# One scaling pass with a running minimum over the scores, and a new order of the work

## The chip, the cores and the metric

One NeuronCore of a Trainium2 chip runs the whole program. The metric is the time of one execution on the device, in microseconds (us); shorter is better. Engines are named as in the profile: PE (TensorE, matrix products; PEld is its weight load), DVE (VectorE), ACT (ScalarE), POOL (GpSimd) and SP (SyncE, which here only issues DMAs).

## The reference

Four batches, eight heads, 576 positions, 64 dimensions per head, all fp32. Queries and keys are rotated by position, then each head is an ordinary softmax attention, and the result goes through a feed-forward network (FFN) with a gate:

```
scores = (1/8) * q_rot @ k_rot^T
scores = scores - max(scores)
attn   = exp(scores) / (sum(exp(scores)) + 1e-9)
x      = attn @ v                                  # heads side by side: 2304 x 512
h      = x @ w_in                                  # 512 -> 2048
out    = (h * clip(h + 3, 0, 6) / 6) @ w_out       # 2048 -> 512
```

## The kernel before

The 2304 rows are cut into 18 tiles of 128 rows; a tile has 8 heads, so there are 144 head-tiles, called heads below. Tile 0 runs in fp32. For the rest every operand is split into a high and a low fp16 part (line 253 or 257 makes the high part, line 265 or 270 the low one), and a product is the sum of three fp16 products: high by high, high by low, low by high.

A head of tiles 1 to 17 (`attention`, line 599) goes through these steps. PE computes the scores S into PSUM, 128 rows by 576 keys (line 570; 573 for the two tiles that lie in two batches). DVE takes the negated maximum of each row (L614). A one-column operation on DVE or POOL turns it into the bias of the exponential, maximum times the row's scale `sig` plus ln 16 (L617). ACT takes the exponential in place, with the sum of the row (L621). ACT or DVE writes its high fp16 part into P16 (L628 or L630), DVE the low part (L632). A DMA issued by SP transposes P16 into PT, and PE multiplies PT by v (L588). S has two buffers in PSUM, P16 four (`NP16`) and PT three (`NPT`). After eight heads `emit_x` divides by the row sums, splits x and transposes it for the FFN.

The FFN works on blocks: tiles 0, 1, 2 and 3 alone, then seven blocks of two tiles. `ffn_h` (L867) computes a slice of h as twelve products in a row, `gate` (L881, L888) applies the gate and splits g (its low part is L898 on POOL), and `ffn_o` (L929) adds six products at a time to the output. The first product of a block of two tiles, the "first wide product" below, has 256 columns where those before have 128; it needs x of tiles 4 and 5. Up to then w_in and w_out are read as 64-bit numbers, decoded on ACT, POOL (L503, L509) and DVE (L517), and split (L265 and others).

All engines run their instructions in the order in which the Python code issues them, and that order is planned. Each step is a generator that yields the engine it wants and an assumed duration; class `Emission` keeps a clock for each engine, lets the waiting step of lowest priority number go first, and chooses for an operation that may run on two engines (`choose`) the one with the smaller sum of queue, duration and a bias from the table `CFG`. `CFG` also holds the priorities and `lead`: a head may be issued only while its number is at most `lead` above the count of FFN units done. So a number in this table, or an assumed duration, changes nothing but the order and the engine.

Of the kernel before, what the change touches and what calls it, by code (L numbers as in the profile page):

```python
# [19 lines left out]
LN_ES = 2.772588722239781  # L20
EPS_ES = 1.6e-8
# [8 lines left out]
NP16 = 4  # L30
NE = 2
# [4 lines left out]
NPT = 3  # L36

CFG = {'a0': 0.5, 'a1': 1, 'a2': 1, 'k1': 0, 'kv': 3, 'q1': 0, 'q': 0, 'wi': 2, 'wo': -0.5, 'gate': -1, 'x': 0, 'lead': 26, 'lat': 0.3, 'dma': 1.2, 'back': 2.0, 'a16': -1, 'v0': 1, 'wb': 0, 'si': 4, 'so': 4, 'bias': [{'loD': -1, 'elD': 20, 'glD': 0.96, 'ehD': 0.18, 'ghD': -0.5, 'ropeD': 2, 'xhD': 0.56, 'xlD': -1.7, 'hiP': 0.0, 'ehP': 0.0, 'ghP': 0.5, 'xhP': 0.03, 'lowP': -4, 'sgP': 0.0, 'hiD': 0.62, 'wboD': 0.0, 'qbD': 0.5, 'biD': 0.0}, {'loD': 0.5, 'elD': 1, 'glD': -1.09, 'ehD': 0.5, 'ghD': 4.88, 'ropeD': 5, 'xhD': -0.07, 'xlD': -1, 'hiP': 0.83, 'ehP': 0.5, 'ghP': -0.24, 'xhP': 0.1, 'lowP': -4, 'sgP': 0.33, 'hiD': 20, 'wboD': 1, 'qbD': -0.77, 'biD': 0.0}, {'loD': -1.94, 'elD': 0.14, 'glD': 5, 'ehD': 0.36, 'ghD': 1.5, 'ropeD': 2.4, 'xhD': 0, 'xlD': 0, 'hiP': 1.5, 'ehP': 2, 'ghP': -4, 'xhP': 5.81, 'lowP': -0.17, 'sgP': 3, 'hiD': 3, 'wboD': -0.5, 'qbD': 3.8, 'biD': 0.46}], 'kvs': 0, 'vpos': 0, 'q0': 'P', 'ch': 1, 'ks': -0.7}  # L40
LAT = CFG["lat"]


class Emission:
# [6 lines left out]

    def __init__(self, tokens):
        self.heap, self.seq, self.clock = [], 0, 0.0
        self.tokens = tokens
        self.busy = {e: 0.0 for e in "DAPE"}
        self.waiting = {e: [] for e in "DAPE"}
        self.dma_free = 0.0
        self.share, self.phase = {}, 0
# [15 lines left out]
    def dma(self, x):  # L74

        self.dma_free = max(self.dma_free, self.clock + 1.35) + x
        return self.dma_free + CFG["dma"]
# [11 lines left out]
    def step(self, gen, prio, end, prev, sent=None):  # L89

        try:
            e, x = gen.send(sent)
        except StopIteration:
            return
        go = lambda t, p=None, s=None: self.post(t, lambda: self.step(gen, prio, t, p, s))
        if e == "N":
            go(end, prev)
        elif e in "UT":
            go(end + x if e == "U" else max(end, x))
        elif e == "S":  # L100
            self.post(end + 0.15, lambda: self.step(gen, prio, self.dma(x), None))
        elif e == "C":
            self.post(end, lambda: self.poll(x, gen, prio, prev))
# [16 lines left out]
    def queue(self, e, x, gen, prio, prev):  # L120
        if e[0] == "X":
            e = self.choose(e[1:], x, prio)
            x = x[e]
        p = min(prio, 0) if e == "E" and prio < 5 else prio

        def add():
            self.seq += 1
            bisect.insort(self.waiting[e], (p, self.seq, x, lambda end: self.step(gen, prio, end, e, e)))
            self.dispatch(e)
        self.post(self.clock + (LAT if e != prev else 0.0), add)  # L130

    def choose(self, kind, x, prio):

        def cost(e):
            ahead = max(self.busy[e] - self.clock, 0.0) + sum(w[2] for w in self.waiting[e] if w[0] <= prio)
            return ahead + x[e] + CFG["bias"][self.phase].get(kind + e, 0.0)
        return min(x, key=cost)

    def dispatch(self, e):
        if self.waiting[e] and self.busy[e] <= self.clock + 1e-6:  # L140
            _, _, dur, go = self.waiting[e].pop(0)
            end = self.busy[e] = self.clock + dur
            go(end)
            self.post(end, lambda: self.dispatch(e))
# [3 lines left out]
def attention_ffn(ctx: ExitStack, tc, q, k, v, w_in, w_out, rope, ident, out):  # L148
# [9 lines left out]
    TT = {"D": 0.61, "P": 1.23}  # L158
    em = Emission({"S": 2, "E": NE, "P16": NP16, "PT": NPT, "av": 1, "x": 1, "h": 2, "tg": 2, "g": NG,
# [28 lines left out]
    def pow2_all(parts, name, scale):  # L188

        yield "D", 0.1  # L190
# [6 lines left out]
        yield "D", 0.6  # L197
# [32 lines left out]
    def rope_steps(x, ti, n, engines, start=None):  # L230
# [7 lines left out]
        e = yield "Xrope", {e: TT[e] for e in engines}  # L238
# [3 lines left out]
        yield e, TT[e]  # L242
# [820 lines left out]
```

## Time and profile before

| | us |
|---|---|
| median of 3 runs | 678.85 (676.17 to 678.94) |
| the profiled execution | 675.35 |
| span of its trace | 673.5 |
| PE busy in the span | 580.8 |
| DVE busy | 477.0 |
| POOL busy | 393.8 |
| ACT busy | 368.6 |

The span goes from the first to the last instruction; the execution's own time is 1.85 us longer. "Busy" of an engine is the time in which it executes. A share of busy time is a mean over stages with different limits, so the rows below are read by stage. The granted clock of PE is given as a share of its full speed of 2.4 GHz; 0.50 is its other level, 1.2 GHz.

### The profile page before, as it was taken

The numbers are of one execution on the slowest core, as the hardware profiler recorded it, in microseconds if no ns is written. First come the engines' busy times: TensorE is split into PE (matmuls) and PEld (weight loads), VectorE is DVE, ScalarE is ACT, GpSimd is POOL, SyncE is SP. The second block draws the span as 40 slices with busy tenths as digits, with TensorE's granted clock in tenths as the row PEclk, the third lists the DMA queues.
The fourth block names the chain that finished last, engine by engine and source line by source line (L and its number), as shares of the span: only waits on it lengthen the run. The fifth ranks groups of instructions, "written<-read, shape, count | busy, mean of one in ns | idle before, by whom it ended". The sixth has DMA issues, their size and how long they took to land.

```text
span 673.5 us, 15004 instructions
## 1 busy us (share of the span) xinstructions
PE 580.8 (86%) x5860; PEld 415.2 (62%) x5860; DVE 477.0 (71%) x780; ACT 368.6 (55%) x665; POOL 393.8 (58%) x481
## 2 busy tenths in 40 slices
PE   1786697487999866999999789989999999999997
PEld 1674574374767533875776357756677677776663
DVE  6999898999776997796678859866675666751110
ACT  3768684647565445476556475755655555542110
POOL 6789799977264793555379845725445362333330
PEclk9989698689799985999999999999999999999999
DMA  8796976578677778765777799587866668441000
GB/s 310 179 289 250 274 203 124 113 125 163 143 137 127 176 168 149 173 133 139 165 152 140 137 185 196 126 165 107 154 112 120 119 136 136 96 114 32 1 16 33
DMA packets 252295, 97.97 MB, mean 145 GB/s; under 512 B 235840, under 2 KB 235968, under 8 KB 252224
## 3 DMA queue, kind: packets, MB, share of 16 engines
q1 hardware_dynamic: 252224, 97.01, 66.7%
q8 instruction: 46, 0.75, 0.5%
q14 instruction: 25, 0.20, 0.1%
HBM read 31.97 MB, written 4.72 MB: 54 GB/s over the span
## 4 chain that ended last, share of the span: by engine, by line
PE 48%; DVE 20%; POOL 11%; DMA 9%; issue 7%; ACT 3%; SPq 1%; POOLq 0%; DVEq 0%; ACTq 0%
PE h L867 20%; PE o L929 17%; DMA PT<-P 5%; PE S L570 5%; PE av L588 5%; DVE P L632 3%; DVE mx L614 2%; POOL ropeA L240 2%; POOL g L898 1%; PE S L573 1%; DVE tg L888 1%; DMA wi_st<-x 1%; POOL g L257 1%; DVE vA L265 1%; DVE vam L209 1%
## 5 line engine op out<-in xcount | busy, mean ns | idle before, releaser
L867 PEld LDWEIGHTS <-wi_st 128*128 128x128 f16 x1920 | 165.2, 99 | 32.2 <-issue 2.7
L929 PE MATMUL o<-wo_st,g 128*128 128x512 f16 x732 | 178.4, 382 | 5.9 <-POOL g L898 4.2
L621 ACT ACTIVATE S<-S,bi,sig 128x576 f32<-128x576 f32 x136 | 108.7, 799 | 104.4 <-POOL bi L617 63.3
L867 PE MATMUL h<-wi_st 128*128 128x256 f16 (+1 forms) x1344 | 145.2, 262 | 1.3 <-DMA wi_st<-x 1.3
L614 DVE TENSOR_REDUCE mx<-S 128x1 f32<-128x576 f32 x136 | 100.9, 752 | 54.7 <-PE S L570 42.4
L632 DVE TENSOR_TENSOR P<-S,P 128x576 f16<-128x576 f32 x136 | 101.2, 752 | 27.5 <-ACT P L628 26.7
L929 PEld LDWEIGHTS <-g 128*128 128x128 f16 x732 | 68.1, 98 | 73.3 <-POOL g L898 7.1
L257 POOL TENSOR_SCALAR g<-tg 128x512 f16<-128x512 f32 x60 | 37.9, 632 | 108.9 <-DVE tg L888 94.4
L588 PEld LDWEIGHTS <-PT 128*128 128x128 f16 (+1 forms) x2128 | 73.9, 103 | 44.5 <-DMA PT<-P 31.4
L570 PE MATMUL S<-kT,qT 128*128 128x288 f16 x480 | 82.6, 304 | 17.7 <-DVE P L632 17.2
L617 POOL TENSOR_SCALAR bi<-mx,sig 128x1 f32<-128x1 f32 x94 | 34.5, 367 | 103.4 <-DVE mx L614 91.5
L881 ACT ACTIVATE tg<-h,g,block_sc 128x512 f32<-128x512 f32 x68 | 52.7, 775 | 75.1 <-PE h L867 74.7
L588 PE MATMUL av<-vA,PT 128*128 128x64 f16 (+1 forms) x1520 | 64.9, 197 | 24.4 <-DMA PT<-P 20.7
L888 DVE SCALAR_TENSOR_TENSOR tg<-tg,h 128x512 f32<-128x512 f32 x68 | 46.5, 683 | 52.2 <-ACT tg L881 51.7
L628 ACT ACTIVATE P<-S 128x576 f16<-128x576 f32 x110 | 70.8, 649 | 2.6
L570 PEld LDWEIGHTS <-qT 128*128 128x128 f16 x480 | 46.2, 102 | 40.2 <-DVE P L632 17.6
L898 POOL TENSOR_TENSOR g<-tg,g 128x512 f16<-128x512 f32 x57 | 68.2, 1197 | 3.4
L867 PE MATMUL h<-xTa,wi_st 128*128 128x256 f16 (+1 forms) x576 | 59.3, 255 | 1.6 <-DMA xTa<-x 1.6
L588 PE MATMUL av<-vB,PT 128*128 128x64 f16 (+1 forms) x608 | 39.5, 197 | 0.0
L630 DVE CAST P<-S 128x576 f16<-128x576 f32 x26 | 19.6, 755 | 11.1 <-ACT S L621 10.4
L621 ACT ACTIVATION_READ_ACCUMULATOR S<-S,bi,sig 128x1 f32 x136 | 26.5, 195 | 0.0
L949 ACT ACTIVATE wo_st<-o,block_sc 128x512 f32<-128x512 f32 x17 | 11.6, 684 | 26.0 <-PE o L929 26.0
(162 smaller groups left out, 819.3 us busy)
## 6 DMA issues: line engine op xcount, KB each, us to landing
raw<-in_w_in SPq DMA_DIRECT2D x16, 512.0 KB, 6.6
raw<-in_w_out SPq DMA_DIRECT2D x16, 512.0 KB, 4.9
qraw<-in_q SPq DMA_DIRECT2D x18, 256.0 KB, 3.3
out<-wo_st SPq DMA_DIRECT2D x17, 256.0 KB, 2.3
kst<-in_k SPq DMA_DIRECT2D x16, 256.0 KB, 4.4
vst<-in_v SPq DMA_DIRECT2D x15, 256.0 KB, 4.4
PT<-P SPq DMA_TRANSPOSE x136, 2.9
vB<-vA SPq DMA_DIRECT2D x8, 256.0 KB, 3.8
```

The lines of the kernel that those rows point to most:

```text
L257: POOL.tensor_scalar(out=out, in0=in_, scalar1=s, scalar2=0.0, op0=ALU.mult, op1=ALU.add)
L570: PE.matmul(out=S[:, j, 0:288], lhsT=qT_t[t][:, o, h, :], rhs=kT_t[b0][:, h, ks], **st)
L588: PE.matmul(out=av[r0:r1, h, :], lhsT=PT[:, blk, r0:r1], rhs=rhs, start=(n == 0), stop=(n == len(terms) - 1))
L614: DVE.tensor_reduce(out=mx, in_=S[:, :, 0:288], axis=AX.XY, op=ALU.max, negate=True)
L621: ACT.activation(out=E, in_=E, func=ACTF.Exp, scale=sig_t[t], bias=bi, accum_out=sum_t[t][:, h:h + 1])
L628: ACT.activation(out=hi, in_=E, func=ACTF.Copy)
L632: DVE.tensor_tensor(out=lo, in0=E, in1=hi, op=ALU.subtract)
L867: PE.matmul(out=h[:, i, :], lhsT=wi_h(p, wl)[:, 256 * c + f0:256 * c + f0 + 128], rhs=xT[:, 4 * xl + c, :], start=(n == 0), stop=(n == 11))
L881: ACT.activation(out=tg, in_=hf, func=ACTF.Relu, scale=osc[j], bias=g3)
L888: DVE.scalar_tensor_tensor(out=whole if j < NF else tg, in0=tg, scalar=6.0 * GAM, in1=hf, op0=ALU.min, op1=ALU.mult)
L898: ENG[e].tensor_tensor(out=gf[:, 1], in0=tg, in1=gf[:, 0], op=ALU.subtract)
L929: PE.matmul(out=os[n][0], lhsT=g[:, gl, mm % nm, 128 * n:128 * n + 128], rhs=wo_h(mm, wl), start=(mm == 0 and gl == 0 and wl == 0), stop=( ...
```

## The change

The maximum over the scores and the bias step are replaced by one DVE pass that multiplies the scores in place by minus `sig` and returns the minimum of each row (the `min` with 3.0e38 changes nothing; it names the operation that the accumulator uses). The exponential then takes scale -1 and that minimum as its bias. The factor 16 of the exponential moves into the two passes that split it. P16 has five buffers instead of four, PT four instead of three, and the tile buffer E of the eight fp32 heads is gone: they use P16's.

The planner gets other durations, a shared port for DVE and POOL (steps marked `d` and `P`), a model of the DMA queue, and a new `CFG` (one line of it below). The FFN products are yielded in threes (three for one accumulation step) where before twelve or six were one step. The planned distance between a transposition and the product that reads it grows: before, the landing was planned 1.35 + 1.0 + 1.2 us after the issue at the earliest, now 1.35 + 1.0 + 0.6 + 1.996.

```diff
-LN_ES = 2.772588722239781
-EPS_ES = 1.6e-8
+ES = 16.0
+EPS = 1.0e-9
-NP16 = 4
-NE = 2
+NP16 = 5
-NPT = 3
+NPT = 4
-CFG = {..., 'lead': 26, 'lat': 0.3, 'dma': 1.2, ...}
+CFG = {..., 'lead': 32, 'lat': 0.008, 'dma': 1.996, ...}
...
-        POOL.tensor_scalar(out=sg, in0=sg, scalar1=2.0 ** -17, scalar2=None, op0=ALU.mult)
+        POOL.tensor_scalar(out=sg, in0=sg, scalar1=-2.0 ** -17, scalar2=None, op0=ALU.mult)
...
-        yield "D", 0.68
-        mx = col("mx", 1, 3)
-        DVE.tensor_reduce(out=mx, in_=S[:, :, 0:288], axis=AX.XY, op=ALU.max, negate=True)
-        e = yield "Xbi", {"D": 0.25, "P": 0.17}
-        bi = col("bi", 1, 3)
-        ENG[e].tensor_scalar(out=bi, in0=mx, scalar1=sig_t[t], scalar2=LN_ES, op0=ALU.mult, op1=ALU.add)
-
-        yield "A", 0.8
-        E = S[:, :, 0:288]
-        ACT.activation(out=E, in_=E, func=ACTF.Exp, scale=sig_t[t], bias=bi, accum_out=sum_t[t][:, h:h + 1])
+        yield "D", 0.88
+        E = S[:, :, 0:288]
+        mx = col("mx", 1, 3)
+        DVE.tensor_scalar(out=E, in0=E, scalar1=sig_t[t], scalar2=3.0e38, op0=ALU.mult, op1=ALU.min, accum_out=mx)
+        yield "A", 0.93
+        ACT.activation(out=E, in_=E, func=ACTF.Exp, scale=-1.0, bias=mx, accum_out=sum_t[t][:, h:h + 1])
...
         if e == "A":
-            ACT.activation(out=hi, in_=E, func=ACTF.Copy)
-        else:
-            DVE.tensor_copy(out=hi, in_=E)
-        yield "D", 0.73
-        DVE.tensor_tensor(out=lo, in0=E, in1=hi, op=ALU.subtract)
+            ACT.activation(out=hi, in_=E, func=ACTF.Copy, scale=ES)
+        else:
+            DVE.tensor_scalar(out=hi, in0=E, scalar1=ES, scalar2=None, op0=ALU.mult)
+        yield "D", 0.75
+        DVE.scalar_tensor_tensor(out=lo, in0=E, scalar=ES, in1=hi, op0=ALU.mult, op1=ALU.subtract)
...
-                    yield "E", (2.68 if N == 128 else 2.63) / nm
                     n = 0
                     for c in range(4):
+                        yield "E", 0.67 / nm
                         for wl, xl in ((0, 0), (0, 1), (1, 0)):
...
-                        yield "E", 1.71 if j < NF else 1.29
                         for mm in (m, m + 1):
+                            yield "E", 0.855 if j < NF else 0.65
```

On DVE, while the keys of the third batch are split (`k` is their fp16 form, `P` is P16, `mx` the column of row maxima, `bi` the bias, `tg` the gate's tile), the order before is:

```order
L614 TENSOR_REDUCE mx<-S 128x1 x2
L617 TENSOR_SCALAR bi<-mx,sig 128x1 x2
L265 SCALAR_TENSOR_TENSOR k_3043<-kst,ks,k_3043 128x8x64
L630 CAST P_3071<-S 128x576
L632 TENSOR_TENSOR P_3071<-S,P_3071 128x576
L632 TENSOR_TENSOR P_3073<-S,P_3073 128x576
L614 TENSOR_REDUCE mx<-S 128x1 x2
L617 TENSOR_SCALAR bi<-mx,sig 128x1
```

and in the changed kernel, at the same place:

```order
L655 TENSOR_SCALAR S,mx<-S,sig 128x2x288
L668 SCALAR_TENSOR_TENSOR P_3103<-S,P_3103 128x576
L668 SCALAR_TENSOR_TENSOR P_3153<-S,P_3153 128x576
L655 TENSOR_SCALAR S,mx<-S,sig 128x2x288 x2
L668 SCALAR_TENSOR_TENSOR P_3204<-S,P_3204 128x576
L302 SCALAR_TENSOR_TENSOR k_3209<-kst,ks,k_3209 128x8x64
L922 SCALAR_TENSOR_TENSOR tg<-tg,h 128x512
```

The bias steps are gone, one pass stands where the maximum stood, and the high part is left to ACT: over the whole program 135 of the 136 high parts are on ACT now, where 110 were.

On POOL, while the weights are decoded and split (`raw` holds their words, `tw` the decoded low part and sign, `wi_st` w_in, `bi` the bias), the order before is:

```order
L617 TENSOR_SCALAR bi<-mx,sig 128x1
L503 TENSOR_SCALAR tw<-raw 128x1024
L330 TENSOR_TENSOR sig<-qp_488,p2k_151 128x1
L331 TENSOR_SCALAR sig<-sig 128x1
L509 TENSOR_SCALAR tw<-raw 128x1024
L503 TENSOR_SCALAR tw<-raw 128x1024
L509 TENSOR_SCALAR tw<-raw 128x1024
L617 TENSOR_SCALAR bi<-mx,sig 128x1
L257 TENSOR_SCALAR wi_st<-wi_st,wsi 128x1024
```

and now:

```order
L277 TENSOR_TENSOR ropeA<-qraw,rope_sb 128x512
L280 TENSOR_TENSOR qraw<-qraw,rope_sb 128x512
L282 TENSOR_TENSOR qraw<-qraw,ropeA 128x512
L541 TENSOR_SCALAR tw<-raw 128x1024 x4
L368 TENSOR_TENSOR sig<-qp_560,p2k_159 128x1
L369 TENSOR_SCALAR sig<-sig 128x1
L541 TENSOR_SCALAR tw<-raw 128x1024 x2
L294 TENSOR_SCALAR wi_st<-wi_st,wsi 128x1024
```

The sign pass (L509 before) is no longer on POOL: its nine instructions there went to ACT. L541 is L503 under its new number. Of six splits of w_in on POOL one is left, and no bias stands among them.

## Rows read from the trace of the kernel before

**Rows 1.** The page's head: span, then busy time and share of two engines.

```profile
span 673.5 us, 15004 instructions
...
PE 580.8 (86%) x5860; PEld 415.2 (62%) x5860; DVE 477.0 (71%) x780; ACT 368.6 (55%) x665; POOL 393.8 (58%) x481
```

**Rows 2.** Busy time by stretch; the second line names the columns.

```profile
core 0: us, PE busy (x) PEld busy (x) DVE busy (x) ACT busy (x) POOL busy (x), PEclk, DMA share, GB/s
...
20.00:140.00 120.00, 84.73 (x581) 64.94 (x580) 111.75 (x154) 81.75 (x135) 108.62 (x86) 0.85 0.76 197
...
174.00:240.00 66.00, 63.30 (x933) 45.53 (x932) 52.24 (x98) 38.70 (x73) 37.39 (x56) 0.99 0.71 144
240.00:266.00 26.00, 14.15 (x147) 8.69 (x145) 21.00 (x34) 13.56 (x27) 17.45 (x18) 0.64 0.81 154
266.00:600.00 334.00, 316.75 (x3367) 227.87 (x3368) 238.19 (x418) 193.79 (x367) 176.78 (x262) 0.99 0.72 142
```

**Rows 3.** PE in order of time around the first wide product: start, duration, instruction, wait.

```profile
262.46 0.71 PE L588 MATMUL av<-vA,PT 128*128 128x64 f16 x10 [2.89 <-DMA PT<-P]
...
266.15 5.11 PE L867 MATMUL h<-wi_st 128*128 128x256 f16 x24 [0.76 <-DMA wi_st<-x]
```

**Rows 4.** PE's waits from 266 us to the end: total us, times, longest.

```profile
PE av L588 <- DMA PT<-P: 5.7, 9, 1.4
PE S L570 <- DVE P L632: 5.0, 4, 2.2
PE o L929 <- POOL g L898: 3.5, 4, 1.7
```

**Rows 5.** Groups by line and shape, whole span: busy us, mean ns, idle before.

```profile
L614 DVE TENSOR_REDUCE mx<-S 128x1 f32<-128x576 f32 x136 | 100.9, 752 | 54.7 <-PE S L570 42.4 <-PE S L573 6.1 <-POOL qraw L245 2.4
...
L617 POOL TENSOR_SCALAR bi<-mx,sig 128x1 f32<-128x1 f32 x94 | 34.5, 367 | 103.4 <-DVE mx L614 91.5 <-ACT P L628 5.0 <-ACT S L621 3.1
...
L199 DVE TENSOR_SCALAR_CACHE_REDUCE chain<-chain 128x128 f32<-128x128 f32 x10 | 2.9, 291 | 5.3 <-PE chain L196 5.3
...
L199 DVE DVE_READ_ACCUMULATOR chain<-chain 128x1 f32 x10 | 1.4, 139 | 0.0
```

**Rows 6.** Two POOL groups of the same view.

```profile
L509 POOL TENSOR_SCALAR tw<-raw 128x1024 f16<-128x1024 f32 x6 | 10.6, 1766 | 0.4
...
L257 POOL TENSOR_SCALAR wi_st<-wi_st,wsi 128x1024 f16<-128x1024 f32 x6 | 8.1, 1350 | 0.1
```

**Rows 7.** DVE groups by line and shape in the first 266 us.

```profile
L265 DVE SCALAR_TENSOR_TENSOR wi_st<-wi_st,wsi 128x1024 f16<-128x1024 f32 x8 | 14.4, 1804 | 0.0
L517 DVE SCALAR_TENSOR_TENSOR wi_st<-wi_st,wo_st 128x1024 uint32<-128x1024 uint32 x8 | 13.3, 1678 | 0.0
...
L265 DVE SCALAR_TENSOR_TENSOR k<-kst,ks,k 128x512 f16<-128x512 f32 x8 | 10.3, 1284 | 0.2 <-ACT k L253 0.2
...
L265 DVE SCALAR_TENSOR_TENSOR wo_st<-wo_st,wso 128x1024 f16<-128x1024 f32 x5 | 9.1, 1815 | 0.2 <-ACT wo_st L253 0.2
L888 DVE SCALAR_TENSOR_TENSOR tg<-tg,h 128x512 f32<-128x512 f32 x12 | 8.2, 680 | 1.8 <-ACT tg L881 1.7
...
L617 DVE TENSOR_SCALAR bi<-mx,sig 128x1 f32<-128x1 f32 x21 | 4.2, 206 | 0.2
```

**Rows 8.** All engines in order of time, 130 to 139 us.

```profile
132.48 4.34 DVE L265 SCALAR_TENSOR_TENSOR wi_st<-wi_st,wsi 128x1024 f16<-128x1024 f32 x2
...
133.51 2.23 POOL L243 TENSOR_TENSOR kst<-kst,rope_sb 128x512 f32<-128x512 f32 x1
...
137.54 1.86 PE L570 MATMUL S<-kT,qT 128*128 128x288 f16 x7 [5.36 <-DVE P L632]
```

**Rows 9.** The same view, 264 to 267 us.

```profile
264.38 0.76 DVE L614 TENSOR_REDUCE mx<-S 128x1 f32<-128x576 f32 x1 [0.19 <-PE S L570]
265.24 0.27 POOL L617 TENSOR_SCALAR bi<-mx,sig 128x1 f32<-128x1 f32 x1 [3.61 <-DVE mx L614]
...
265.54 0.80 ACT L621 ACTIVATE S<-S,bi,sig 128x576 f32<-128x576 f32 x1 [2.13 <-POOL bi L617]
```

More of the change, by code (lines that the diff above doesn't have):

```diff
@@ L72, in free, with dma, land @@
         self.tokens[name] += 1
-    def dma(self, x):
-        self.dma_free = max(self.dma_free, self.clock + 1.35) + x
-        return self.dma_free + CFG["dma"]
+    def dma(self, x, kind="S", then=None):
+        at = max(self.clock, self.issue_free)
+        self.issue_free = at + self.ISSUE[kind]
+        self.dma_free = max(self.dma_free, at + 1.35) + x
+        d = {"at": at, "land": self.dma_free + self.LAND[kind], "done": False, "then": [then] if then else []}
+        before, self.last = self.last, d
+        def land():
+            t = d["land"] = max(d["land"], before["land"] + 0.8) if before else d["land"]
+            if t > self.clock + 1e-6:
+                self.post(t, land)
+                return
+            d["done"] = True
+            for fn in d["then"]:
+                fn(t)
+        self.post(d["land"], land)
+        return d
     def when(self, cond, fn):
@@ L94, in step @@
             return
+        if prev == "E" and e != "E":
+            end += 0.17
         go = lambda t, p=None, s=None: self.post(t, lambda: self.step(gen, prio, t, p, s))
@@ L97, in step @@
             go(end, prev)
[L98 to L101, printed above, removed]
+        elif e == "U":
+            go(end + x)
+        elif e == "T":
+            if x["done"]:
+                go(end)
+            else:
+                x["then"].append(lambda t: self.step(gen, prio, max(t, end), None))
+        elif e in "SZ":
+            self.post(end + 0.05, lambda: self.dma(x, e, lambda t: self.step(gen, prio, t + CFG["dma"], None)))
         elif e == "C":
-            self.post(end, lambda: self.poll(x, gen, prio, prev))
+            self.post(end, lambda: self.poll(x, gen, prio, None))
         elif e == "R":
@@ L127, in add @@
             self.seq += 1
-            bisect.insort(self.waiting[e], (p, self.seq, x, lambda end: self.step(gen, prio, end, e, e)))
+            bisect.insort(self.waiting[e], (p, self.seq, x, port, lambda end: self.step(gen, prio, end, e, e)))
             self.dispatch(e)
-        self.post(self.clock + (LAT if e != prev else 0.0), add)
+        self.post(self.clock + (self.WAKE[e] + CFG["lat"] if e != prev else 0.0), add)
     def choose(self, kind, x, prio):
         def cost(e):
-            ahead = max(self.busy[e] - self.clock, 0.0) + sum(w[2] for w in self.waiting[e] if w[0] <= prio)
-            return ahead + x[e] + CFG["bias"][self.phase].get(kind + e, 0.0)
+            E = e.upper()
+            ahead = max(self.busy[E] - self.clock, 0.0) + sum(w[2] for w in self.waiting[E] if w[0] <= prio)
+            if e in "dP":
+                ahead = max(ahead, self.port - self.clock - self.PORT[E])
+            return ahead + x[e] + CFG["bias"][self.phase].get(kind + E, 0.0)
         return min(x, key=cost)
@@ L140, in dispatch @@
         if self.waiting[e] and self.busy[e] <= self.clock + 1e-6:
-            _, _, dur, go = self.waiting[e].pop(0)
-            end = self.busy[e] = self.clock + dur
+            _, _, dur, port, go = self.waiting[e].pop(0)
+            end = self.clock + dur
+            if port:
+                pre = min(self.PORT[e], dur)
+                end = self.port = max(self.clock + pre, self.port) + dur - pre
+            self.busy[e] = end - min(self.LEAD[e], 0.5 * dur)
             go(end)
-            self.post(end, lambda: self.dispatch(e))
+            self.post(self.busy[e], lambda: self.dispatch(e))
 @with_exitstack
@@ L188, in pow2_all @@
     def pow2_all(parts, name, scale):
-        yield "D", 0.1
+        yield "D", 0.16
         pm = col("pm", 1, 2)
@@ L704, in attention_first @@
         free("h")
-        free("E")
+        free("P16")
         if h == 0:
@@ L761, in emit_first @@
     def emit_first():
-        yield "D", 0.3
+        yield "D", 0.35
         r = col("rsum", 8, 2)
-        DVE.tensor_scalar(out=r, in0=sum_t.pop(0), scalar1=EPS_ES, scalar2=None, op0=ALU.add)
+        DVE.tensor_scalar(out=r, in0=sum_t.pop(0), scalar1=EPS, scalar2=None, op0=ALU.add)
         DVE.reciprocal(out=r, in_=r)
@@ L792, in emit_x @@
         r = col("rsum", 8, 2)
-        DVE.tensor_scalar(out=r, in0=sum_t.pop(t), scalar1=EPS_ES, scalar2=None, op0=ALU.add)
+        DVE.tensor_scalar(out=r, in0=sum_t.pop(t), scalar1=EPS, scalar2=ES, op0=ALU.add, op1=ALU.mult)
         DVE.reciprocal(out=r, in_=r)
```

119 lines of the change are left out of this document (63 added, 56 removed).

## The prediction

> **What bounds the kernel now.** I read the page's head first, then busy time by stretch, then PE's waits, and the groups by line last. PE is busy 580.8 of 673.5 us, far ahead of the other engines [rows 1], so the question is in which stretches PE is not fed. The stretches divide the run at the first wide product, at 266 us. From 20 to 140 us PE is busy 84.7 of 120 at a granted clock of 0.85, while DVE works 111.8 and POOL 108.6: the two set the pace. From 174 to 240 PE is full (63.3 of 66) and DVE idles 13.8. From 240 to 266 PE is starved: 14.2 of 26 us busy, mean clock 0.64, DVE 21.0 of 26. From 266 to 600 PE is busy 316.75 of 334, so 17.25 us are idle; DVE has 95.8 to spare there [rows 2]. The reader is to see two regimes: ahead of 266 the time is set by when DVE gets tile 5 through, since the first wide product waits for the transposed x of it (a product with v waits 2.89 us for its PT, and the wide product itself 0.76 us for x) [rows 3]; behind 266 it is PE's own work plus its idle time.
>
> So the sum has two terms: how much earlier the first wide product starts, and how much idle time behind it goes. Work on PE is the same in both kernels, product for product.
>
> **Part 1: the scores' pass.** Per head a maximum of 752 ns goes, and a bias of 367 ns (94 on POOL) or 206 ns (the DVE ones in the first stretch) [rows 5, 7]. The new pass is not in this trace in its size. Its nearest kin is L199, the same kind of instruction with an accumulator over 128 columns of PSUM: 291 ns, and 139 ns for the read of the accumulator [rows 5]. From L199 to the 576 columns of L614 it is 448 columns and 461 ns, 1.03 ns each. At that rate the new pass takes 291 + 461 + 139 = 0.89 us, 0.14 more than the maximum. Bounds: 0.75 (the read hidden behind the next instruction) and 1.35 (448 more columns at twice the time each). I take 0.89, since L199 shows both instructions. ACT's work for the exponential is the same.
>
> DVE up to x of tile 5, counted in the two orders: 42 passes by 0.14 are +5.8; 21 biases by 0.206 are -4.3; the high parts fall from 7 to 1, by 0.75 each -4.5. The other moves between engines go against DVE there: 3 more low splits of w_out by 1.815 are +5.4 [rows 7]; 13 high parts of k, q, v and w_in and three rotation steps come to it, 7 steps on x and g and five copies leave it. Priced alike at the 0.68 of a 512-column step [rows 7], these 16 less 12 are +2.7. Net about +5, and I hold 0 to +10 for possible.
>
> What becomes shorter is the way from maximum to exponential. A maximum ends at 265.14, the bias on POOL runs from 265.24 to 265.51, the exponential starts at 265.54 [rows 9]: 0.4 us, of which a hand-over of about 0.1 stays and the accumulator's read comes in. Where POOL is in the middle of a longer step it costs more. In the starved stretch and in the one around 130 us I take 3 us for it (0 to 6). Elsewhere it is hidden behind PE's other work.
>
> **Part 2: POOL and DVE in each other's way.** In the first 266 us DVE steps on two SBUF operands are long for their size. A 512-column gate step takes 680 ns, so 1024 columns would take 0.68 + 512 x 1.03 ns = 1.21; but the splits of w_in take 1.804 (8), the decoding 1.678 (8), the splits of w_out 1.815 (5), and 512-column splits of k 1.284 (8) [rows 7]. The excess is 4.8 + 3.7 + 3.0 + 4.8 = 16.3 us. It falls together with POOL's work: two splits took 4.34 us while POOL's rotation beside them took 2.23, and in that time PE waited 5.36 us for a low part that stands behind the splits on DVE [rows 8]. POOL loses, before the keys of batch 1 are rotated, 9 sign passes by at most 1.77, four splits of w_in by 1.35 and six biases by 0.37 [rows 5, 6]: 23.5 of its 108.6 us, about a fifth. A fifth to a third of 16.3 is 3 to 5; I take -5 (0 to -16). ACT takes the sign passes over: it is busy 81.8 of 120 us there [rows 2], which is the cover; without it the decoding would end some of those 16 us later.
>
> **Part 3: the order.** This is the main term. By the two orders, PE has issued at the first product of block 3 the scores of 37 heads and products with v of 34; in the changed kernel 43 and 40. At the first wide product they are 54 and 50, against 55 and 51. So six heads are moved from the starved stretch (240 to 266) into one in which DVE idles 13.8 us and PE is full. Six heads are on DVE 6 x (0.75 + 0.75 + 0.2) = 10.2 us, which fit into the 13.8. I take -10 (0 to -14). What is late next is DVE itself, which is near full up to tile 5. PE's low clock goes with the starving and is no term of its own.
>
> First wide product: +5 - 3 - 5 - 10 = -13 us.
>
> **Part 4: behind 266 us.** PE waits 5.7 us for PT, 5.0 for low parts that free S, 3.5 for g on POOL [rows 4]: 14.2 of the 17.25. The order before was planned with 0.68 for a maximum that takes 0.752; a step planned too short puts the reader too early, and everything behind it on PE stands still. Now the assumed durations agree with the rows, a product with v is planned at least 1.4 us further behind its transposition, five P16 and four PT hold what is then in flight, and scores can come in after three FFN products instead of six or twelve. Switching between h and o costs nothing to speak of by the counts: the same products in smaller turns. SP issues the same DMAs, so no queue grows. I take -11 (-14 to +6, since a new order can form waits of its own).
>
> **Sum.** 675.35 - 13 - 11 = 651.35 for an execution like the profiled one. That one lies 3.5 us below the median of the runs; the median to expect is 655.
>
> **The rivals.**
>
> A smaller gain: DVE sets the time of tile 5, and its work up to there does not fall. For it: its sum is level to slightly higher, and it was busy 93% of the stretch from 20 to 140 [rows 2]. Against it: 13.8 us of idle time lie right ahead of the starved stretch. Then the first term is nought, the second stays: 675.35 - 11 + 3.5 = 668 (663 to 675).
>
> A larger gain: the excess of part 2 goes altogether and DVE's idle time up to 266 is filled. Then the first term is 5 - 3 - 16.3 - 13.8 = -28, the second at most -14.2: 675.35 - 42 + 3.5 = 637 (625 to 642). Against it: POOL keeps four fifths of its early work. The Trainium skill, SBUF — State Buffer, section "Who interferes with whom", says that a DVE instruction with two SBUF inputs and a GpSimd instruction that reads SBUF exclude one another for a whole instruction, not in shares. By that rule, the trace agrees (1.804 against 1.21 for the same columns), and each step taken off POOL in the right place would give back a whole step of waiting.
>
> No change: the waits come back at other places, in the same amount, as the new order is planned by a model as the old one was. For it: nothing on PE becomes less. 675.5 to 682.
>
> Slower: the new pass takes twice the time per column, since it reads and writes PSUM in place and also accumulates; no row shows one that long. At 1.6 us it adds 0.71 x 42 = 30 us to DVE ahead of 266, against 24 us won in all, and behind 266 the remaining 94 heads add 67 us to DVE's 238 of 334, so that half of the gain there goes: 675.35 + 30 - 13 - 5 + 3.5 = 691. It decides from about 1.46 us on, where 0.57 x 42 uses up the 24. Against it: L199 also writes PSUM in place, and runs at 1.03 ns per column.
>
> **How the numbers follow.** The forecast has 0.52, with a range of its own from 643 to 664. The smaller gain has 0.19, the larger 0.11, no change 0.08, slower 0.10. A measurement of this kernel tells from no change what is over 0.5%, that is, outside 675.5 to 682.2. Faster is then 0.52 + 0.19 + 0.11 = 0.82. The range of 8 in 10 leaves out the lower half of the larger gain and the slower case: 633 to 681.
>
> **What would show it.** In the changed profile: L655 with its read at 0.85 to 0.95 us a head; DVE's splits of w_in nearer 1.5 than 1.8; the first wide product at about 253 instead of 266; PE fuller in the 26 us ahead of it, at a clock near 1; idle time of PE behind it about 6 of 330 us, with PT nearly gone from its waits. The forecast is wrong if the wide product starts no earlier, if L655 is over 1.4 us, or if PE behind it waits over 15 us.

## The result, and the profile after

| | before | after |
|---|---|---|
| median of 4 runs, us | 678.03 (676.17 to 678.94) | 657.2 (654.6 to 658.88) |
| ratio of the times (95% interval) | | 0.9693 (0.9653 to 0.9733) |
| the profiled execution's own time, us | 675.35 | 654.6 |
| start of the first wide product, us | 266.15 | 249.59 |
| from there to the end of the span, us | 407.35 | 403.11 |
| heads through DVE's low part by 240 us | 36 | 42 |

The changed kernel is 3.1% faster; 655 was forecast. The profiled executions differ by 20.75 us. The first wide product comes 16.6 us earlier (forecast 13), and what lies behind it is 4.2 us shorter (forecast 11). Single executions of the kernel before range from 670.9 to 682.7 us over all measurements here, so two or three microseconds between two profiles are not yet a finding.

The page's head of the changed kernel, which answers to [rows 1]:

```profile
span 652.7 us, 14935 instructions
...
PE 573.3 (88%) x5860; PEld 410.8 (63%) x5860; DVE 447.6 (69%) x844; ACT 386.2 (59%) x715; POOL 322.2 (49%) x363
```

POOL has 71.6 us less to do, ACT 17.6 more. DVE has 29.4 us less although the accumulator's reads brought it more instructions. Busy time by stretch, with the columns of [rows 2]:

```profile
20.00:140.00 120.00, 85.04 (x602) 65.32 (x602) 109.40 (x170) 92.00 (x148) 66.20 (x62) 0.85 0.79 199
...
174.00:240.00 66.00, 59.83 (x919) 43.62 (x918) 53.09 (x119) 43.29 (x86) 38.29 (x46) 1.00 0.98 173
240.00:266.00 26.00, 24.83 (x278) 17.92 (x276) 14.85 (x25) 14.65 (x28) 15.76 (x18) 1.00 0.91 153
266.00:600.00 334.00, 322.67 (x3393) 230.04 (x3392) 220.61 (x456) 197.85 (x389) 159.57 (x192) 1.00 0.75 139
```

The starved stretch from 240 to 266 us is full now: PE is busy 24.83 of 26 us at a granted clock of 1.00, where it had 14.15 at 0.64. From 20 to 140 us POOL works 66.2 us instead of 108.6. PE around the first wide product, against [rows 3]: the product with v ahead of it waits 0.24 us for its PT instead of 2.89, and the wide product itself waits for nothing. From 266 to 600 us PE is idle 11.3 us, where it was 17.25 and about 6 were forecast.

```profile
248.68 0.47 PE L626 MATMUL av<-vA,PT 128*128 128x64 f16 x10 [0.24 <-DMA PT<-P]
...
249.59 0.82 PE L901 MATMUL h<-wi_st 128*128 128x256 f16 x6
```

PE's waits from 249.59 us to the end, against [rows 4]:

```profile
PE av L626 <- DMA PT<-P: 6.6, 8, 1.6
PE S L608 <- DVE P L668: 3.0, 4, 1.3
PE o L963 <- ACT wo_st L983: 1.6, 1, 1.6
PE o L963 <- POOL wo_st L294: 1.3, 1, 1.3
PE o L963 <- POOL wo_st L932: 0.8, 2, 0.6
PE o L963 <- POOL g L932: 0.7, 2, 0.5
```

The wait for low parts fell from 5.0 to 3.0 us. That for g on POOL fell from 3.5 to 2.8 us; parts of g now lie where w_out's stage was (`wo_st`, L294 and L932), and these waits are counted here. (L294 makes a high part; a wait of 0.4 us for one, on g in the kernel before, is not in the 3.5.) L983 is the output's copy. The wait for PT did not go: 6.6 us in 8 waits, where it had been 5.7 in 9. Of the 14.2 us of these three, 12.4 are still there. Two waits of the kernel before have gone, on transposed x. The second ends where the first wide product starts:

```profile
PE h L867 <- DMA xTa<-x: 1.6, 1, 1.6
...
PE h L867 <- DMA wi_st<-x: 0.8, 1, 0.8
```

Groups by line and shape over the whole span, which answer to [rows 5, 7]; L302 is the low part's line, L555 the decoding:

```profile
L655 DVE TENSOR_SCALAR_CACHE_REDUCE S<-S,sig 128x576 f32<-128x576 f32 x136 | 109.6, 819 | 31.1 <-PE S L608 25.3 <-PE S L611 5.4 <-POOL sig L369 0.2
L655 DVE DVE_READ_ACCUMULATOR S<-S,sig 128x1 f32 x136 | 19.0, 140 | 0.0
L657 ACT ACTIVATE S<-S,mx 128x576 f32<-128x576 f32 x136 | 96.9, 713 | 100.9 <-DVE S L655 99.1 <-DVE rsum L827 1.6
L302 DVE SCALAR_TENSOR_TENSOR wi_st<-wi_st,wsi 128x1024 f16<-128x1024 f32 x8 | 12.2, 1540 | 0.0
L555 DVE SCALAR_TENSOR_TENSOR wi_st<-wi_st,wo_st 128x1024 uint32<-128x1024 uint32 x8 | 9.7, 1230 | 1.3 <-ACT wo_st L549 0.9 <-issue 0.4
L302 DVE SCALAR_TENSOR_TENSOR wo_st<-wo_st,wso 128x1024 f16<-128x1024 f32 x8 | 10.6, 1324 | 0.0
L292 DVE TENSOR_SCALAR wo_st<-kst,ks 128x512 f16<-128x512 f32 x3 | 2.4, 835 | 0.0
```

The record of the new pass is 819 ns long and that of its read 140. They overlap: the read starts 82 ns before the pass ends (median), so both together take 0.88 us a head. The exponential, thought unchanged, takes 713 ns where [rows 9] show one of 0.80 us. The splits of w_in, the decoding of w_in and the splits of w_out fell from 1804, 1678 and 1815 ns to 1540, 1230 and 1324. All 16 sign passes [rows 6] are on ACT.

### The profile page after: what moved, and what is told of

It is laid out like the page before. It is cut to its first block, busy times and chain, and to the rows that moved or that the text cites. A ratio compares the mean times of both kernels' runs of the same rounds, so it can differ in the third digit from the quotient of the medians.

```text
span 652.7 us, 14935 instructions
## 1 busy us (share of the span) xinstructions
PE 573.3 (88%) x5860; PEld 410.8 (63%) x5860; DVE 447.6 (69%) x844; ACT 386.2 (59%) x715; POOL 322.2 (49%) x363
## 4 chain that ended last, share of the span: by engine, by line
PE 52%; POOL 14%; DVE 11%; DMA 9%; issue 7%; ACT 6%; SPq 1%; POOLq 0%; DVEq 0%; ACTq 0%
PE o L963 20%; PE h L901 17%; DMA PT<-P 6%; PE av L626 5%; PE S L608 5%; POOL ropeA L277 3%; POOL kst L280 3%; POOL kst L282 3%; DVE P L668 2%; DVE S L655 2%; PE S L697 2%; DVE tg L922 1%; PE S L611 1%; PE av L747 1%; DMA raw<-in_w_out 1%
## 5 line engine op out<-in xcount | busy, mean ns | idle before, releaser
L901 PE MATMUL h<-wi_st 128*128 128x256 f16 (+1 forms) x1344 | 162.3, 259 | 1.1 <-DVE tg L922 0.7
L657 ACT ACTIVATE S<-S,mx 128x576 f32<-128x576 f32 x136 | 96.9, 713 | 100.9 <-DVE S L655 99.1
L655 DVE TENSOR_SCALAR_CACHE_REDUCE S<-S,sig 128x576 f32<-128x576 f32 x136 | 109.6, 819 | 31.1 <-PE S L608 25.3
L668 DVE SCALAR_TENSOR_TENSOR P<-S,P 128x576 f16<-128x576 f32 x136 | 100.9, 752 | 31.7 <-ACT P L664 31.2
L294 POOL TENSOR_SCALAR g<-tg 128x512 f16<-128x512 f32 x44 | 28.0, 637 | 182.0 <-DVE tg L922 172.3
L664 ACT ACTIVATE P<-S 128x576 f16<-128x576 f32 x135 | 85.6, 647 | 1.8
L626 PE MATMUL av<-vA,PT 128*128 128x64 f16 (+1 forms) x1520 | 64.9, 197 | 21.1 <-DMA PT<-P 20.1
L932 POOL TENSOR_TENSOR g<-tg,g 128x512 f16<-128x512 f32 x58 | 67.4, 1162 | 8.8 <-ACT g L290 5.3
L963 PE MATMUL o<-wo_st 128*128 128x512 f16 x120 | 32.7, 380 | 2.3 <-POOL wo_st L294 1.3
L277 POOL TENSOR_TENSOR ropeA<-kst,rope_sb 128x512 f32<-128x512 f32 (+1 forms) x16 | 20.9, 1308 | 13.7 <-DMA kst<-in_k 13.0
L841 POOL TENSOR_TENSOR x<-x,x 128x512 f16<-128x512 f32 x15 | 18.3, 1217 | 17.9 <-ACT x L290 17.9
L657 ACT ACTIVATION_READ_ACCUMULATOR S<-S,mx 128x1 f32 x136 | 26.6, 196 | 0.0
```

Source lines behind the costliest of these rows:

```text
L277: ENG[e].tensor_tensor(out=v4(ta), in0=x4[:, :, ::-1, :], in1=sinb.to_broadcast([n, 8, 2, 32]), op=ALU.mult)
L626: PE.matmul(out=av[r0:r1, h, :], lhsT=PT[:, blk, r0:r1], rhs=rhs, start=(n == 0), stop=(n == len(terms) - 1))
L655: DVE.tensor_scalar(out=E, in0=E, scalar1=sig_t[t], scalar2=3.0e38, op0=ALU.mult, op1=ALU.min, accum_out=mx)
L657: ACT.activation(out=E, in_=E, func=ACTF.Exp, scale=-1.0, bias=mx, accum_out=sum_t[t][:, h:h + 1])
L664: ACT.activation(out=hi, in_=E, func=ACTF.Copy, scale=ES)
L668: DVE.scalar_tensor_tensor(out=lo, in0=E, scalar=ES, in1=hi, op0=ALU.mult, op1=ALU.subtract)
```

## The experiments

Two theories stood at the start. One: the order makes the gain, by bringing the heads of tile 5 through DVE sooner, and the new pass itself is worth little. The other: the pass makes it. Times are medians, ratios are to the kernel before on the same chip. Its median was 678.03 us beside the changed kernel and 675.6 to 677.1 beside the others, so the ratios compare better than the times do. The last three columns are read from the profiled executions, one for each kernel.

| what runs | us | ratio (95%) | heads by 240 us | first wide product | from there to the end |
|---|---|---|---|---|---|
| before | 678.03 | 1 | 36 | 266.2 | 407.4 |
| after | 657.2 | 0.969 (0.965 to 0.973) | 42 | 249.6 | 403.1 |
| after's order, old steps, bias on DVE | 666.36 | 0.986 (0.983 to 0.989) | 40 | 257.9 | 408.7 |
| after's order, old steps, bias on POOL | 685.25 | 1.014 (1.010 to 1.018) | 38 | 264.4 | 420.3 |
| before's order, new pass | 672.96 | 0.994 (0.991 to 0.997) | 38 | 264.0 | 407.0 |
| after's order, scale from a column | 658.59 | 0.973 (0.968 to 0.977) | 42 | 251.0 | 406.4 |
| after's order, sign passes on POOL | 668.43 | 0.988 (0.985 to 0.991) | 38 | 263.3 | 402.8 |
| after with the old table | 682.1 | 1.008 (1.005 to 1.012) | 37 | 263.6 | 417.4 |
| distance to the product 0.6 | 679.87 | 1.007 (1.004 to 1.010) | 37 | 261.8 | 419.5 |
| distance to the product 3.4 | 683.13 | 1.012 (1.006 to 1.018) | 39 | 258.1 | 424.2 |
| FFN products in twelves and sixes | 677.94 | 1.004 (1.001 to 1.007) | 38 | 262.9 | 414.1 |
| pause 0.020 instead of 0.008 | 673.71 | 0.996 (0.992 to 0.999) | 37 | 264.6 | 408.4 |
| four P16, three PT | 659.97 | 0.976 (0.970 to 0.983) | 40 | 255.3 | 403.7 |
| loads and stores issued by ACT | 674.55 | 0.998 (0.995 to 1.000) | 38 | 269.6 | 407.5 |

### The pass in the changed order

The steps are those of before, in the changed kernel's order, instruction for instruction (`sig` keeps its plus sign, too):

```diff
-        DVE.tensor_scalar(out=E, in0=E, scalar1=sig_t[t], scalar2=3.0e38, op0=ALU.mult, op1=ALU.min, accum_out=mx)
+        DVE.tensor_reduce(out=mx, in_=E, axis=AX.XY, op=ALU.max, negate=True)
+        bi = col("bi", 1, 3)
+        DVE.tensor_scalar(out=bi, in0=mx, scalar1=sig_t[t], scalar2=None, op0=ALU.mult)
...
-        ACT.activation(out=E, in_=E, func=ACTF.Exp, scale=-1.0, bias=mx, ...)
+        ACT.activation(out=E, in_=E, func=ACTF.Exp, scale=sig_t[t], bias=bi, ...)
```

> The changed kernel, in its own order instruction for instruction, but with the old steps for the scores: maximum and bias on DVE, the exponential with the row's scale read from a column. The result is unchanged. Theory (the order makes the gain): DVE takes 752 + 207 ns a head instead of 819 + 140, the same, so the time stays within 3 us of the changed kernel's 657.2: 656 to 661. Rival (the pass makes the gain, by one step less on the way to the exponential and an exponential of 713 instead of 799 ns): at least half of the 20.8 us goes back, 668 or more.

Measured: 666.36 us, 9.2 above the changed kernel, or 11 by the ratios. That lies between the two forecasts: the steps are worth about half of the gain. In the run with the old steps, two heads in a row on DVE and the first of them on ACT:

```profile
309.75 0.75 DVE L655 TENSOR_REDUCE mx<-S 128x1 f32<-128x576 f32 x1
...
310.54 0.21 DVE L657 TENSOR_SCALAR bi<-mx,sig 128x1 f32<-128x1 f32 x1
310.67 0.75 DVE L655 TENSOR_REDUCE mx<-S 128x1 f32<-128x576 f32 x1
310.85 0.80 ACT L659 ACTIVATE S<-S,bi,sig 128x576 f32<-128x576 f32 x1 [1.46 <-DVE bi L657]
```

and in the changed kernel, to be held beside [rows 9] too:

```profile
332.10 0.81 DVE L655 TENSOR_SCALAR_CACHE_REDUCE S<-S,sig 128x576 f32<-128x576 f32 x1
...
332.83 0.13 DVE L655 DVE_READ_ACCUMULATOR S<-S,sig 128x1 f32 x1
332.83 0.81 DVE L655 TENSOR_SCALAR_CACHE_REDUCE S<-S,sig 128x576 f32<-128x576 f32 x1
333.00 0.71 ACT L657 ACTIVATE S<-S,mx 128x576 f32<-128x576 f32 x1 [0.17 <-DVE S L655]
```

The durations add up to the same on DVE (750 + 214 ns for maximum and bias, 819 + 140 now), and the expectation went by these sums. But instructions on DVE overlap. The next head's pass starts 0.73 us after this one, and 0.92 us with the old steps. Over all cases in which DVE had its next step ready, the medians are 0.74 us (95 heads) and 0.91 us (98 heads); in the kernel before, a step starts 0.67 us after the maximum (87 heads), with most biases on POOL. DVE is busy 463.1 us in this run and 447.6 in the changed kernel. An estimate from these: 0.17 us for each of the 46 heads whose pass lies ahead of the first wide product are 8 us, as much as that product moved (8.3).

The way to the exponential is shorter as well. From the start of the pass to its start it is 0.90 us instead of 1.10 here, and 0.17 less in the mean over 136 heads; the exponential itself is 0.09 shorter. These 0.26 us a head are 35 us over all heads, of which 9 to 11 reach the time. How the gain divides between DVE's time and the shorter way, no run separates.

### The bias on POOL, and the pass in the old order

The first of these differs from the run above in one word (`POOL.tensor_scalar` for the bias). The second is the kernel before with the new pass alone: its planner still plans a bias step, for which nothing is issued.

> As the run before, but the bias of every head on POOL, where 94 of 136 were before the change. Theory (order): the way from maximum to exponential grows by about 0.3 us a head and by POOL's queue; ahead of the first wide product that costs up to 4 us, behind it PE's other work hides most of it: 658 to 664. Rival (pass): 670 or more, since this is the step that the change took out.

> The kernel before, in its own order, with the new pass alone in place of maximum and bias (the factor 16 in the two splitting passes); the result is unchanged. Theory (order): the first wide product comes 0 to 3 us earlier, the rest stays, 673 to 678. Rival (pass): at least half of the gain, 667 or less.

Measured: 685.25 and 672.96 us. With the bias on POOL a head waits for a third engine's queue, and the changed order has no room for it: 28 us above the changed kernel, slower than before. DVE's load is not the reason: it is busy 440.3 us, less than in the changed kernel, while the exponential starts 1.75 us after the maximum, in the mean, instead of 1.20. In the old order the same new pass is worth only 0.6%. So "what the pass is worth" has no single answer: 4 us in the one order, 9 to 28 in the other, by what it replaces. Neither of the two theories holds alone. By the ratios the order without the pass gains 1.4%, the pass without the order 0.6%, and both together 3.1%.

### What shortened the exponential

```diff
-        ACT.activation(out=E, in_=E, func=ACTF.Exp, scale=-1.0, bias=mx, ...)
+        ACT.activation(out=E, in_=E, func=ACTF.Exp, scale=neg1, bias=mx, ...)   # neg1: a 128x1 column of -1
```

> The order of the changed kernel, instruction for instruction; only the exponential reads its scale (-1) from a 128x1 column instead of taking it as a constant. In the changed kernel the exponential takes 713 ns, in the run with the old steps in this order (scale from a column) 802 ns. Theory: the column costs those 89 ns, so the exponential is at 800 ns here, and of the 9 us that the old steps cost in this order a part comes from ACT: 659 to 664 us. Rival: the exponential is shorter because the pass ahead of it has rewritten S, and the scale has no part in it: 713 ns and 656 to 658 us.

The group of it in this run:

```profile
L658 ACT ACTIVATE S<-S,mx,neg 128x576 f32<-128x576 f32 x136 | 108.8, 800 | 97.9 <-DVE S L656 96.2 <-DVE rsum L828 1.6
```

The scale read from a column costs 87 ns, the whole difference. The time rises by 1.4 us, inside the intervals of both and short of the 659 to 664 us that were expected. The Trainium skill, ScalarE: Activation LUTs, section "What ACT_TABLE_LOAD costs", gives about 93 ns for each one-column operand of an ACTIVATE; the measured 87 agree, and the forecast should have counted it.

### POOL and DVE in each other's way

The changed kernel runs the 16 sign passes of the decoding on ACT. Here they run on POOL, everything else in its place:

```diff
-        if e == "P":
+        if e in "PA":
             POOL.tensor_scalar(out=sign, in0=w1, scalar1=2.0 ** -60, ...)
```

> The order of the changed kernel on PE, DVE and SP; only the 16 sign passes of the weight decoding run on POOL instead of ACT, in their place. That gives POOL some 21 us back and takes 22 us off ACT ahead of the first wide product. Theory (POOL and DVE are in each other's way, part 2 of the prediction): DVE's splits of w_in go from 1540 ns back to about 1800 and the decoding from 1230 to about 1680, and the first wide product comes 5 to 10 us later: 662 to 668 us. Rival: the DVE steps are long for another reason (their own operands, the DMAs), they stay within 100 ns of 1540 and 1230, and the time is 655 to 659 us. If only the steps grow and the time stays, the contention is real and costs nothing here.

Measured: 668.43 us, 11 above the changed kernel. In the profiled executions the first wide product comes 13.7 us later and the rest is 0.4 us shorter. The page's head and the groups on DVE:

```profile
PE 580.3 (87%) x5860; PEld 415.9 (62%) x5860; DVE 457.1 (69%) x844; ACT 367.2 (55%) x699; POOL 345.9 (52%) x379
```

```profile
L302 DVE SCALAR_TENSOR_TENSOR wi_st<-wi_st,wsi 128x1024 f16<-128x1024 f32 x8 | 14.2, 1787 | 0.0
...
L555 DVE SCALAR_TENSOR_TENSOR wi_st<-wi_st,wo_st 128x1024 uint32<-128x1024 uint32 x8 | 10.6, 1340 | 2.6 <-POOL wo_st L547 2.6
...
L292 DVE TENSOR_SCALAR wo_st<-kst,ks 128x512 f16<-128x512 f32 x3 | 4.5, 1564 | 0.0
```

The same 844 instructions of DVE take 9.5 us longer when POOL does 23.7 us more. The splits of w_in are back at 1787 ns as the theory said. The decoding rose only by 110 ns, where the theory had 450, and the splits of w_out stayed at 1324. A step with a single SBUF operand (L292, 835 ns in the changed kernel) went to 1564. So the price in DVE's time is real, and it is paid by whichever step POOL happens to lie beside.

It is not shown to be the whole delay. Up to the first wide product DVE is busy 9.2 us longer and idle 4.5 us longer, and a cause that the expectation left out shows on ACT. The exponentials of the eight fp32 heads wait for their bias (L708), which stands on POOL behind the sign passes. The wait up to the first wide product, in the changed kernel and then in this run:

```profile
ACT E L712 <- POOL bi L708: 0.8, 1, 0.8
```

```profile
ACT E L712 <- POOL bi L708: 10.6, 4, 5.6
```

The last of these exponentials starts at 69.9 us instead of 60.4. Part of the 13.7 us thus comes from POOL's own queue, and how much is open.

### The planner's numbers

Five runs change numbers that only set the order. First the old table in the changed kernel, and the planned distance between a transposition and its product either way (`'dma': 1.996` to 0.6 and to 3.4):

> The changed kernel with its pass, its assumed durations, its model of the port and its threes, but the table of biases, priorities, lead and DMA margin of the kernel before. Theory (order, and in it the table): most of the gain goes, 670 to 680, with POOL busier ahead of the first wide product and that product at about 260 us. Rival (the assumed durations and the port model carry it, the table is a detail): 663 or less.

> The changed kernel with the margin behind a transposition put back to the distance of before: 0.6 us instead of 1.996, so that a reader is planned 3.55 us after the issue at the earliest instead of 4.95. Theory (the distance saves waits on PT): PE's waits for PT grow from 20.1 us by 10 or more, and the time by 3 to 8, to 660 to 665. Rival (a transposition lands when the queue lets it, and a head further behind only moves the wait): waits for PT the same within 4 us, 655 to 659.

> The changed kernel with the margin behind a transposition at 3.4 us instead of 1.996. Theory (distance saves waits): PE's waits for PT fall from 20.1 to below 12, and the time stays or falls by up to 4 us, 653 to 658. Rival (buffers end it: with four PT and five P16 a reader further behind holds them longer, and low parts and scores wait): waits for PT fall, but the time rises to 660 or more.

Then the FFN products planned in twelves and sixes again (`yield "E", 2.68 / nm` once in place of four times 0.67, and 1.71 or 1.3 in place of halves), and the buffers of before (`NP16 = 4`, `NPT = 3`):

> The changed kernel with the FFN products planned in groups of twelve and six again. Theory of the prediction (threes let scores and products with v in earlier and take idle time from PE behind the first wide product): 2 to 5 us slower, 659 to 662. Rival (the same products in larger turns cost PE nothing, since the attention is not the late one behind the first wide product): 655 to 659.

> The changed kernel with four P16 and three PT as before the change. Theory (the buffers are needed for the greater distance): 3 to 8 us slower, 660 to 665, with DVE's low parts later and PE waiting longer for them. Rival (three PT are enough, since a PT is held for about 5 us and a head comes every 4): 655 to 659.

Measured: 682.1, 679.87, 683.13, 677.94 and 659.97 us. The extra buffers matter little: the difference of 2.8 us (5 by the ratios) lies within the intervals. Each of the other four alone undoes the whole gain. For the short distance and for the threes neither forecast of the time held; both came out about 15 us above it. The distance does what it should to the wait that it is meant for. PE's largest wait behind the first wide product, with the short distance:

```profile
PE av L626 <- DMA PT<-P: 19.0, 22, 4.2
```

and the two largest with the long one:

```profile
PE S L608 <- DVE P L668: 13.2, 10, 6.4
PE av L626 <- DMA PT<-P: 5.5, 2, 4.5
```

Too near, and PE waits for PT; too far, and the wait turns into one for low parts that free S. Both also lose 8 to 12 us ahead of the first wide product. With the long distance PE's waits for low parts show it there too (21.1 us, 10.1 in the changed kernel); with the short one PE waits no longer for PT there (12.5 us against 13.5), and still the wide product comes 12 us later. That four unlike changes all land at 678 to 683 raised the question whether the gain belongs to the numbers or to this one order. A change that stands for nothing answers it:

```diff
-'lat': 0.008
+'lat': 0.02
```

> One constant of the planner, the pause that it assumes between two engines, goes from 0.008 to 0.020 us: 12 ns, less than the resolution of anything that it stands for. The order that comes out differs on all engines. Theory: the gain sits in this one order, which the numbers of the table were fitted to, and any other order out of the same planner loses much of it, as the changes of the product's distance, of the grouping and of the table did: 668 to 683 us. Rival: each of those numbers had an effect of its own, 12 ns have none: 655 to 660 us.

Measured: 673.71 us. Twelve nanoseconds of assumed pause give another order on every engine, and about four fifths of the gain are gone. So the four runs before this one do not show what their numbers are worth either, since each has another order too. 37 heads are through DVE by 240 us instead of 42, and the first wide product comes at 264.6. The low parts of P (L668) up to 240 us, in the changed kernel and then in this run; busy time and count on DVE stand behind the window:

```profile
0.00:240.00 240.00, 31.09 (x42) 0.91 0.86 194
```

```profile
0.00:240.00 240.00, 27.05 (x37) 0.90 0.78 183
```

Most of the gain hangs on an order that was found together with these numbers. The run with fewer buffers is the exception: another order too, 40 heads, and 660 us. What spared it stays open.

### The wait for PT that did not go

In the changed kernel the longest of those waits follows five loads of v on SP's queue. SP, the low part and PE, in order of time:

```profile
267.58 2.48 SPq L451 DMA_DIRECT2D vst<-in_v  x5
269.87 0.74 DVE L668 SCALAR_TENSOR_TENSOR P<-S,P 128x576 f16<-128x576 f32 x1
270.67 2.00 SPq L674 DMA_TRANSPOSE PT<-P  x1
...
277.62 0.47 PE L626 MATMUL av<-vA,PT 128*128 128x64 f16 x10 [1.62 <-DMA PT<-P]
```

P is ready at 270.61 and its transposition is issued at once, but its product can only start 7.0 us later. In four of the eight waits the transposition stood 1.1 to 2.2 us behind another transfer on SP. So the loads of q, k and v and the stores (76 transfers in the trace, not 66) are issued by ACT here:

```diff
-        SP.dma_start(out=x, in_=q[t])
+        ACT.dma_start(out=x, in_=q[t])
...
-        SP.dma_start(out=out[128 * t:128 * t + 128], in_=ob)
+        ACT.dma_start(out=out[128 * t:128 * t + 128], in_=ob)
```

> The order of the changed kernel on PE, DVE and POOL; only the loads of q, k and v and the stores of the output (66 transfers) are issued by ACT instead of SP, so that SP's queue holds transpositions and little else. In the changed kernel the eight waits for PT behind the first wide product (6.6 us) belong to transpositions that stood 1.1 to 2.2 us behind another transfer on SP, or landed 5.4 to 6.9 us after their P beside loads just issued. Theory: the place in SP's queue makes them; the waits for PT behind go to 3 us or less and the time to 650 to 655 us. Rival: the transfers meet in the DMA engines whoever issues them, waits for PT stay at 5 to 8 us and the time at 656 to 660 us. Third: ACT is held by the issuing and by the waits for free buffers, over 660 us.

Measured: 674.55 us, the third outcome. ACT is held by the issuing, from the first microsecond:

```profile
0.71 2.44 ACTq L384 DMA_DIRECT2D kst<-in_k  x5
...
5.74 7.06 ACTq L451 DMA_DIRECT2D wo_st<-in_v  x5
12.83 1.28 ACT L247 ACT_TABLE_LOAD   x1 [12.83 <-DMA raw<-in_w_in]
```

Five loads of v occupy ACT's queue for 7.06 us beside the loads of w_in that SP now issues ahead of time; SP had issued the same five in 3.91 us. ACT loads its tables at 12.83 us instead of 0.71 and begins on the keys at 14.12 instead of 5.97; PE's first product starts at 16.35 instead of 9.27. That is 7 of the 20 us by which the first wide product is late; where the other 13 come from stays open. Behind it the waits for PT are 4.9 us in 8 times, neither gone nor as before. The place on SP's queue is thus at most a part of them; a run that takes the loads off SP without holding ACT was not tried.

## Why the prediction came out right, and where it did not

**What bounds the kernel.** Right: two regimes, divided by the first wide product. The table of runs bears out what the reading rested on. By 240 us six heads more are through DVE, as many as part 3 counts, and of all orders the two with 42 heads come first to the wide product; the one with 36 is the last but one.

**Part 1, the pass.** The price of 0.89 us is near the measured 0.88, by two errors that cancel: from L199 to the new pass it is 1.18 ns a column, not 1.03 (that rate was read between two different instructions, so L199 did not show it), and pass and read overlap by 0.08 us. What went wrong is that durations were added on DVE as if each step waited for the one before to end: the next step starts 0.74 us after the new pass and 0.67 after the old maximum, so a head costs DVE 0.07 us more and not 0.14. On the way to the exponential 3 us were booked for two stretches; over all heads the exponential starts 1.20 us after the pass instead of 2.11, in the mean, and takes 87 ns less, where it was held to be the same. The forecast's own terms for the pass alone are +5.8 and -4.3 on DVE and -3 on the way, a gain of 1.5 us ahead of the first wide product. The profiles give 2.2 in the old order, which is not clear of their spread, and 8.3 in the new one, where all biases stand on DVE.

**Part 2, contention.** The mechanism was right for the splits of w_in, and -5 too small. By the forecast's own count (1.21 us for 1024 columns, 0.68 for 512) the excess fell from 16.3 to 7.5 us: 8 splits of w_in by 0.33, 8 of w_out by 0.11, 8 decodings by 0.02, and 7 splits of k by 0.54 (1217 ns). That is 9 us of DVE time, and taking the sign passes alone back to POOL gave DVE 9.2 us more to do ahead of the first wide product. That the splits of w_out grew shorter through POOL's smaller load is not shown, since they did not come back in that run. The rule that stood with the larger gain, the Trainium skill's in SBUF — State Buffer, "Who interferes with whom", also counts plain `tensor_scalar` steps among those that can be blocked; the trace agrees (L292 went from 835 to 1564 ns).

**Part 3, the order.** Right in count (six heads), wrong in place: they were not all moved into the idle time of 174 to 240 us, where DVE is busy only 0.85 us more. Two heads were gained up to 140 us, two from 140 to 174, two from 174 to 240. The low parts of P on DVE, by stretch:

```profile
0.00:140.00 140.00, 11.00 (x15) 0.87 0.81 216
140.00:174.00 34.00, 5.97 (x8) 0.89 0.82 147
174.00:240.00 66.00, 14.11 (x19) 1.00 0.98 173
```

against, in the kernel before:

```profile
0.00:140.00 140.00, 9.57 (x13) 0.87 0.78 214
140.00:174.00 34.00, 4.47 (x6) 0.90 0.80 150
174.00:240.00 66.00, 12.61 (x17) 0.99 0.71 144
```

So the order's -10 and the pass and the contention are not terms beside each other. The order is the way in which shorter steps become earlier heads. It did not work by filling DVE's idle time, as the -10 had it. Of the 16.6 us by which the first wide product comes earlier, DVE's busy time up to it makes 14.8 (228.71 to 213.95 us), which was forecast level (+5 and -5); its idle time makes 1.8 (37.4 to 35.6). That the first term came out near (-13, measured -16.6) is luck in good part: what was booked as level fell, and the idle time that was to go stayed.

**Part 4, behind the first wide product.** This is the step that failed in size as well: -11 forecast, -4.2 measured, and a run in the same order (scale from a column) has 406.4 us there, so the 4.2 are uncertain by some 3. (The 14.2 us of waits were read to the end of the span, the 17.25 of idle time only to 600; to the end PE's idle time went from 21.9 to 18.3 us.) Of the three waits that it was to end, 14.2 us, 12.4 are left: low parts 3.0, g 2.8, and PT not less but more (5.7 to 6.6). The forecast rested on a greater planned distance and on "SP issues the same DMAs, so no queue grows". The planned distance grew by 1.4 us, but a transposition now lands later. Its line in the kernel before and after, from issue to landing:

```profile
DMA to landing us min/median/max: 2.8/2.9/6.2
```

```profile
DMA to landing us min/median/max: 3.2/3.4/6.9
```

From the issue to its product the median over the heads behind the first wide product went from 4.84 to 5.24 us (worked out from the starts of 94 and 93 pairs): 0.40 more, against 0.5 more to land. The margin is the same, and so is the wait. The rival "no change", in which waits come back elsewhere, lies nearer to this stretch than the forecast does: the waits for low parts fell by 2.3 us (with L573, 0.3 before), that for xTa by 1.6 and that for g by 1.1, while those for PT and for the output's copy (0.8 before) grew by 0.9 and 0.8. The smaller gain (668) had DVE's work up to tile 5 level, and it fell. The larger gain (637) was nearer on contention, which gave 8.8 of the 16.3 us where the forecast took 5, and wrong about DVE's idle time, which was not filled. The slower case needed a pass of 1.46 us, which the 0.88 rule out.

**What stays open.** Why a transposition lands later: it is 3.4 to 3.7 us in every kernel made from the changed one, 3.0 in the one with the old order and the new pass, and neither the table, the distance nor the buffers moves it. And what part of an order's time is its place in a spread that no part of the change explains: 12 ns were worth 16 us.

## What to carry to other kernels

A statically planned order is a fit: judge an edit inside an unchanged order first (same instructions, one thing replaced), because re-planning after the smallest edit can move the time as much as the edit is worth. Count the progress of the work that the bound waits for (here: heads through DVE by a fixed time), not the sum of separately priced parts. On an engine whose records overlap, read a step's price from the distance between starts and not from the sum of durations. Where steps of one engine grow while another works beside it, look for work of that other engine that a third can take.

## What the runs showed of the hardware

A `tensor_scalar` with an accumulator, in place over 128x576 fp32 in PSUM, takes 819 ns and its read 140, so 1.18 ns a column beyond the 291 ns of 128 columns [rows 5]. The read starts 82 ns before the record of the pass ends, and the next DVE step 0.74 us after the pass began. An exponential of the same size takes 713 ns with a constant scale, 800 with a scale column. POOL work laid beside DVE cost DVE 9.5 us for 23.7. Issued from ACT, the first five loads of k (four of 256 KB and one of 128) held its queue for 2.44 us and five loads of v of 256 KB for 7.06 beside other loads; issued from SP in the changed kernel the same loads took 2.47 and 3.91 us.
